# A sketched-attention and tanh-MLP kernel: loads of the last two batches held to half the bytes under way, and a new order on every engine

## The chip, the cores and the metric

The kernel runs on one core of a Trainium2 chip. The metric is the time of one execution on the device, in microseconds (us). Engines are named as the profile names them: PE is the matrix engine (PEld its weight loads), DVE the vector engine, ACT the scalar engine, POOL the GpSimd engine, SP the engine that asks for most transfers; DMA moves data between device memory and the on-chip memory, and PSUM is the memory of eight banks that matmuls write to.

## The reference

Two stages, cut to what matters. Shapes: q, k and v are 4 batches x 4 heads x 1088 positions x 32; the MLP takes 4352 tokens of 128 numbers through 2048 and back.

```python
def phi(x):                                    # S1, S2: 8 x 32
    a = einsum('rd,bhsd->bhsr', S1, x)
    b = einsum('rd,bhsd->bhsr', S2, x)
    return einsum('bhsi,bhsj->bhsij', a, b).reshape(..., 64)

q_p, k_p = phi(q), phi(k)
kv  = einsum('bhsf,bhsd->bhfd', k_p, v)
num = einsum('bhsf,bhfd->bhsd', q_p, kv)
den = einsum('bhsf,bhf->bhs', q_p, sum(k_p, axis=2))[..., None] + 1e-6
x   = (num / den).transpose(0, 2, 1, 3).reshape(4352, 128)
h   = x @ w_in                                 # 128 -> 2048
out = (h - tanh(h)) @ w_out                    # 2048 -> 128
```

## The kernel before

**Work.** A batch goes through these steps. Its k is transposed on DVE (`kT`), projected on PE by both sketches (L524), transposed back on DVE (`kab`, L534), and multiplied out to 64 features on POOL (`wk`, L567); PE forms a Gram matrix and a fold from it (L546, L556), by which the denominator comes out of the query projection, and then the sums over v (L593, or L652 for batches 2 and 3 in one). q is transposed (`qT`, L678), projected (L698), brought back (`qf`, L705) and turned into scaled features by DVE and POOL (`dt`, `den`, `rec`, `an`, `qp`, L711 to L734) and transposed again (`qpT`, L739). The numerators (L754) are matmuls of those with the sums; ACT copies the result as bf16 to `xT` (L771), which holds tokens along its columns.

The MLP takes tokens in twelve groups: 128, 128, 256, seven of 512, 128 and 128. For each 128 of the 2048 hidden units and a group of 512, one matmul of 512 columns writes h to one of the PSUM banks 4 to 6 (0 to 2 as well for the last groups) (L962), ACT makes tanh(-h) of it in bf16 (L968), and a second matmul adds its product with `w_out` to the output's bank 7 (L990). The linear part h @ w_out is not taken through the hidden units: `w_in @ w_out` is formed once (L933), split in two bf16 halves `whi` and `wlo`, and two matmuls (L1013) add x times them to the same bank. DVE moves a finished group's bank to `osb` (L1027), and SP stores it (L1034). Batch 0's first 256 tokens have a shorter way of their own (L782 to L874) so that the MLP can start early; matmuls on zeros (L1110), called fillers below, stand among these steps.

**Order.** The kernel records every step as an `Op` with its engine, its readers and writers, and from these finds the waits. The order on each engine is not worked out at build time: it is the table `ORDER`, a list of the numbers of the ops for each engine, and a negative number in PE's list stands for that many fillers (of 512 columns below -1000, else of 256). Each engine goes through its list in order and stops at an op whose input is not there, so everything that is listed behind it waits too. SP's list holds loads and stores alike.

**Loads.** `load` (L407) adds a rule of its own to each load by SP: going back over the loads that were recorded before it, it adds up bytes until its own and theirs exceed `AHEAD`, 1.9 MB, and makes the load wait for the landing of the one at which that happens. So at most about 1.9 MB is asked for and not landed. A due time goes with each load: below 20000 for batches 0 and 1 and the weights, 20000 to 40020 for k, v and q of batches 2 and 3. One k or q of a batch is 544 KB; v comes in four parts, three of 144 KB and one of 112 KB. k, q and v of batch 2 use the buffers of batch 0, those of batch 3 the buffers of batch 1.

Of the kernel before, what the change touches and what calls it, by code (L numbers as in the profile page):

```python
# [21 lines left out]
AHEAD = 1900000  # L22

ORDER = {
    "tensor": (
# [16 lines left out]
    ),  # L42
    "scalar": (
# [8 lines left out]
    ),  # L52
    "vector": (
# [5 lines left out]
    ),  # L59
    "gpsimd": (  # L60
        3, 20, 21, 4, 9, 22, 7, 8, 10, 75, 84, 82, 60, 59, 61, 62, 135, 133, 147, 148, 146, 283, 285, 305, 308, 306,
        309, 304, 307, 440, 442, 576, 578,
    ),
    "sync": (
# [4 lines left out]
    ),  # L69
}  # L70

# [256 lines left out]
def bass_polysketch_attn__then__act_tanh_shrink_kernel(nc, q, k, v, S1, S2, moe_w_in, moe_w_out, out):  # L328
# [78 lines left out]
    def load(eng, key, sem, due, fn, nbytes, also=False, rate=300, name="load"):  # L407

        o = P.op(eng, nbytes / rate, fn, w=() if also else key if isinstance(key, list) else [key], sem=sem, due=due,
                 name=name)  # L410
        if also:
            P.also(o, key)
        if eng == "sync":
            ahead, i = nbytes, len(flow)
            while i and ahead <= AHEAD:
                i -= 1
                ahead += flow[i][1]
            if ahead > AHEAD:
                landed[0] |= {flow[i][0]}
            o.deps |= landed[0]  # L420
            flow.append((o, nbytes))

    def load_s():
        for i, src in enumerate((S2, S1)):
            load("scalar", ("s_raw",), "s", 0, lambda e, i=i, src=src: e.dma_start(
                out=s_raw[8 * i:8 * i + 8, :, :], in_=src[:, None, :].to_broadcast([R, H, D])), 4096, True, name="load s")

    def load_k(b, due):
        cuts = ((0, 512), (512, S)) if b == 0 else ((0, S),)
        for x, (lo, hi) in enumerate(cuts):  # L430
            load("sync", [("kraw", b % 2, y) for y in ((x,) if b == 0 else (0, 1))], f"k{b}{x}", due, lambda e, lo=lo, hi=hi: e.dma_start(
                out=kraw[b % 2][:, lo:hi], in_=k[b].rearrange("h (j c) d -> (h j) (c d)", j=32)[:, lo:hi]),
                512 * (hi - lo), rate=400, name=f"load k{b}")

    def load_v(b, due):
        src = v[b].rearrange("h (j c) d -> j h c d", j=32)
        for x, c in enumerate((0, 2, 1, 3)):
            n = NT if c < 3 else 7
            load("scalar" if b == 0 and x % 2 else "sync", ("vx", b % 2), f"v{b}{c}", due + x, lambda e, c=c, n=n: e.dma_start(
                out=vx[b % 2][32 * c:32 * c + 32, :, 0:n, :].rearrange("j h t d -> j h (t d)"),  # L440
                in_=src[:, :, OFF[c]:OFF[c] + n, :].rearrange("j h t d -> j h (t d)")),
                128 * 128 * n, True, 226, name=f"load v{b}")
# [696 lines left out]
```

## Time and profile before

| | us |
|---|---|
| median of three runs | 106.21 |
| lowest and highest | 105.36 and 106.97 |
| the profiled execution, its own time | 105.88 |
| its span, from first to last instruction | 103.9 |
| PE busy in it | 94.4 |
| ACT busy in it | 81.5 |

The profile is of one execution. Line numbers (L962) are those of the kernel before. A row of the timeline gives the start, the length, the engine, the line, the operation with what it writes and reads, how many follow each other, and in brackets how long the engine sat idle ahead and what ended that. "issue" there means that the engine waited for nothing that the profile shows. PE's busy time counts matmuls whose ends are modelled and overlap, so a busy PE is not one at its fastest. In the list of transfers q1 is SP's queue and the kind "instruction" is the engines' own code being brought in.

### The profile page before, as it was taken

To read this page: it belongs to the slowest core of one execution; us is meant where nothing else is said; L and a number is where in the kernel's file an instruction comes from. 1 tells how busy PE (TensorE), PEld (TensorE's weight loads), DVE (VectorE), ACT (ScalarE), POOL (GpSimd) and SP (SyncE) were. 2 spreads that over 40 slices of the span, in tenths; PEclk is the share of its full clock that TensorE was granted. 3 is DMA by queue.
4 is the path that set the end of the run, shared out by engine and by line. 5 is a ranking of instruction groups with operands and counts; after the bars stand their busy time and mean duration, and the time that the engine had idled before them with its cause. 6 is when DMAs were issued, how large, how long until landed. Compare 5 with 4: busy or idle time off the path is not lost.

```text
span 103.9 us, 3200 instructions
## 1 busy us (share of the span) xinstructions
PE 94.4 (91%) x1353; PEld 51.9 (50%) x1364; DVE 56.4 (54%) x108; ACT 81.5 (78%) x173; POOL 32.9 (32%) x37
## 2 busy tenths in 40 slices
PE   5989998959689999999999999999999999999980
PEld 1336767737376444444845444344444323454770
DVE  3389879999595988069995307875320020020210
ACT  0528929725857979799689799999799999999960
POOL 5309042799300399995650000091000000000000
PEclk9999999999999999999999999999999999999999
DMA  2999999799962710033000420041005106014053
GB/s 46 318 246 397 396 347 248 246 239 271 284 203 65 193 23 0 6 51 50 6 0 3 73 32 0 14 66 27 0 6 81 20 9 92 0 21 69 14 84 68
DMA packets 22493, 11.21 MB, mean 108 GB/s; under 512 B 17872, under 2 KB 20304, under 8 KB 22480
## 3 DMA queue, kind: packets, MB, share of 16 engines
q1 hardware_dynamic: 21968, 10.69, 40.7%
q10 hardware_dynamic: 512, 0.34, 1.2%
q8 instruction: 10, 0.16, 0.7%
q14 instruction: 3, 0.02, 0.1%
HBM read 8.79 MB, written 2.23 MB: 106 GB/s over the span
## 4 chain that ended last, share of the span: by engine, by line
PE 50%; ACT 28%; DVE 6%; DMA 6%; SPq 3%; issue 3%; DVEq 0%
ACT tt L968 27%; PE ps L962 15%; PE ps L990 14%; DMA w_in_f<-in_moe_w_in_dram 6%; PE ps L754 6%; PE ps L698 3%; PE ps L1013 2%; PE ps L652 2%; PE ps L997 2%; DVE qpT L739 1%; SPq L452 1%; DVE kT L576 1%; PE ps L593 1%; PE ps L524 1%; PE ps L868 1%
## 5 line engine op out<-in xcount | busy, mean ns | idle before, releaser
L968 ACT ACTIVATE tt<-ps 128x512 bf16<-128x512 f32 x136 | 69.0, 685 | 6.8 <-PE ps L962 4.1
L962 PE MATMUL ps<-xT,w_in 128*128 128x512 bf16 (+2 forms) x184 | 42.1, 317 | 1.2 <-issue 0.7
L990 PE MATMUL ps<-tt,w_out 128*128 128x512 bf16 (+2 forms) x158 | 40.1, 336 | 1.8 <-issue 1.7
L962 PEld LDWEIGHTS ps<-xT,w_in 128*128 128x128 bf16 x192 | 18.0, 114 | 17.8 <-ACT tt L968 9.8
L990 PEld LDWEIGHTS ps<-tt,w_out 128*128 128x128 bf16 x160 | 14.2, 98 | 14.1 <-ACT tt L968 2.7
L1027 DVE STREAM_TRANSPOSE osb<-ps 128x512 f32<-128x512 f32 (+2 forms) x10 | 6.1, 605 | 26.3 <-PE ps L990 26.3
L734 POOL TENSOR_TENSOR qp<-an,qf 128x768 f32<-128x768 f32 (+1 forms) x8 | 11.7, 1458 | 25.3 <-DVE an L725 25.0
L567 POOL TENSOR_TENSOR wk<-kab 128x768 f32<-128x768 f32 x10 | 15.1, 1514 | 4.8 <-DVE kab L534 3.9
L739 DVE STREAM_TRANSPOSE qpT<-qp 128x768 f32<-128x768 f32 (+1 forms) x12 | 10.5, 903 | 0.8 <-POOL qp L734 0.8
L705 DVE STREAM_TRANSPOSE qf<-ps 128x1152 f32<-128x1152 f32 (+1 forms) x4 | 5.3, 1316 | 6.0 <-PE ps L698 6.0
L771 ACT CAST xT<-ps 128x272 bf16<-128x272 f32 (+2 forms) x12 | 4.0, 372 | 3.6 <-PE ps L754 3.4
L754 PE MATMUL ps<-qpT,ndw 32*32 32x272 f32 (+3 forms) x256 | 6.0, 385 | 0.3 <-ACT sw L583 0.3
L678 DVE STREAM_TRANSPOSE qT<-qraw 128x1088 f32<-128x1088 f32 (+2 forms) x5 | 5.3, 1062 | 0.5 <-DMA qraw<-in_q_dram 0.5
L1110 PE MATMUL ps<-wz 128*128 128x256 bf16 (+1 forms) x23 | 5.5, 373 | 0.0
L754 PEld LDWEIGHTS ps<-qpT,ndw 32*32 32x32 f32 x256 | 3.2, 103 | 2.5 <-DVE ndw L671 0.4
L1013 PE MATMUL ps<-xT,wlo 128*128 128x512 bf16 (+2 forms) x10 | 3.4, 338 | 1.1 <-DVE wlo L938 0.9
L898 POOL CAST w_out<-w_out_f 128x512 bf16<-128x512 f32 x4 | 2.4, 612 | 5.9 <-DMA w_out_f<-in_moe_w_out_dram 5.8
L771 DVE CAST xT<-ps 128x272 bf16<-128x272 f32 (+1 forms) x4 | 1.8, 511 | 4.5 <-ACT xT L771 2.3
L698 PE MATMUL ps<-qT,sw 32*32 32x288 f32 (+1 forms) x128 | 3.7, 399 | 0.1
L534 DVE STREAM_TRANSPOSE kab<-ps 128x288 f32<-128x288 f32 (+2 forms) x10 | 3.4, 391 | 0.6 <-PE ps L524 0.5
L1110 PEld LDWEIGHTS ps<-wz 128*128 128x128 bf16 x23 | 2.4, 114 | 2.4 <-issue 2.1
L734 DVE TENSOR_TENSOR qp<-ps,qf 128x768 f32<-128x768 f32 (+1 forms) x4 | 3.5, 881 | 0.0
(104 smaller groups left out, 79.0 us busy)
## 6 DMA issues: line engine op xcount, KB each, us to landing
kraw<-in_k_dram SPq DMA_DIRECT2D x3, 544.0 KB, 5.8
qraw<-in_q_dram SPq DMA_DIRECT2D x3, 544.0 KB, 5.4
vx<-in_v_dram SPq DMA_DIRECT2D x11, 144.0 KB, 5.3
out_dram<-osb SPq DMA_DIRECT2D x17, 64.0 KB, 2.0
w_in_f<-in_moe_w_in_dram SPq DMA_DIRECT2D x4, 256.0 KB, 5.8
w_out_f<-in_moe_w_out_dram SPq DMA_DIRECT2D x4, 256.0 KB, 5.7
qraw<-in_q_dram SPq DMA_DIRECT2D x1, 416.0 KB, 5.3
vx<-in_v_dram SPq DMA_DIRECT2D x3, 112.0 KB, 4.4
```

What stands on the lines that cost most here:

```text
L567: P.op(eng, dve(64 * n) if eng == "vector" else pool(64 * n), lambda e: e.tensor_tensor(out=wk[i][:, t0:t1, :, :, :].rearrange("p t h i j ...
L698: ins = e.matmul(ps[32 * c:32 * c + 32, h, 0:N], sw[32 * h:32 * h + 32, b, :], qT[i][32 * h:32 * h + 32, o:o + N], start=True, stop=True, ...
L734: e.tensor_tensor(out=qp[u][:, 4 * lo:4 * hi, :, :], in0=(pa if head else an[u][:, 4 * lo:4 * hi, :])[:, :, :, None].to_broadcast([128, m, ...
L739: P.op("vector", dve(64 * m), lambda e, lo=lo, hi=hi: e.transpose(out=qpT[u][:, :, 32 * lo:32 * hi].rearrange("p x (n j) -> p x n j", j=32 ...
L754: ins = e.matmul(ps[32 * h:32 * h + 32, c, 0:n], ndw[i][32 * c:32 * c + 32, y, 32 * h:32 * h + 32], qpT[u][32 * c:32 * c + 32, 2 * h + y, ...
L771: e.tensor_copy(dst, src) if on == "vector" else e.copy(dst, src), r=[bank[c]],
L962: ins = e.matmul(bk[:, n * y:n * y + n], w_tile(jb), xT[:, t0:t0 + n], start=True, stop=True)
L968: P.op("scalar", act(512), lambda e, ts=ts, bk=bk: e.activation(out=tt[:, ts, :], in_=bk, func=AF.Tanh, scale=-1.0), r=[kb], w=[("t", ts)] ...
L990: ins = e.matmul(acc[:, 0:n], w_out[:, jb, :], tt[:, ts, n * y:n * y + n], start=o.start and y == 0, stop=o.stop and y == per - 1)
L1013: P.op("tensor", 3 + n / 2.4, lambda e, o, x=x: e.matmul(acc[:, 0:n], x[:, :], xT[:, t0:t0 + n], start=o.start, stop=o.stop), r=[(nm,)] + ...
L1027: P.op("vector", dve(n), lambda e: e.transpose(out=osb[u][:, 0:n], in_=acc[:, 0:n]), r=[ka], w=[("osb", u, 0), ("osb", u, 1)], due=when(t0 ...
L1110: P.emit(lambda e, n: e.matmul(ps[:, 6, 0:n], wz[:, 0:128], wz[:, 0:n], start=True, stop=True))
```

## The change

Two things are changed. In `load`, the limit on the bytes under way is `AHEAD` for loads with a due time below 20000, as before, and half of it, 0.95 MB, for the others. And the table `ORDER` is a different one on every engine; 11 more fillers of 256 columns stand in PE's list. The steps themselves, their sizes and their engines are the same. The lines of the changed kernel stand one further down from L413 on.

```diff
         if eng == "sync":
             ahead, i = nbytes, len(flow)
-            while i and ahead <= AHEAD:
+            most = AHEAD if due < 20000 else AHEAD // 2
+            while i and ahead <= most:
                 i -= 1
                 ahead += flow[i][1]
-            if ahead > AHEAD:
+            if ahead > most:
                 landed[0] |= {flow[i][0]}
             o.deps |= landed[0]
             flow.append((o, nbytes))
```

Two lines of the table, PE's first:

```diff
-        2, -1005, -3, 47, -3, 65, 50, 80, -1, 68, -1, 69, -5, 94, 73, 93, 86, 103, 105, 96, 95, -5, 99, 124, 101, 110,
+        2, -1005, -3, 47, -3, 50, 65, 80, -3, 68, -1, 69, -4, 94, 73, -1, 103, 86, -1, 105, 95, 96, 93, -3, 124, 99,
```

What that makes of the order is shown at three places. The first is PE's list ahead of the first tanh: the last transposes of w_in (L920 before, L921 after), key sums of batch 0 (`wk,vx`), fillers (`wz`), query projection (`qT,sw`), the first numerators (`qpdT,kvd`), the turn of the sums (`ident,kvz`) and the first layer (`xT,w_in`). Before:

```order
L829 MATMUL ps<-qT,sw 32x256 x4
L920 MATMUL ps<-identb,w_in 128x128 x16
L811 MATMUL ps<-wk,vx 32x64 x16
L1110 MATMUL ps<-wz 128x256 x5
L868 MATMUL ps<-qpdT,kvd 32x128 x8
L698 MATMUL ps<-qT,sw 32x224 x16
L868 MATMUL ps<-qpdT,kvd 32x128 x8
L962 MATMUL ps<-xT,w_in 128x128 x12
L882 MATMUL ps<-ident,kvz 128x128 x2
```

After:

```order
L921 MATMUL ps<-identb,w_in 128x128 x8
L830 MATMUL ps<-qT,sw 32x256 x4
L1111 MATMUL ps<-wz 128x256
L921 MATMUL ps<-identb,w_in 128x128 x8
L812 MATMUL ps<-wk,vx 32x64 x28
L1111 MATMUL ps<-wz 128x256 x3
L699 MATMUL ps<-qT,sw 32x224 x16
L869 MATMUL ps<-qpdT,kvd 32x128 x16
L1111 MATMUL ps<-wz 128x256 x10
L883 MATMUL ps<-ident,kvz 128x128 x2
L963 MATMUL ps<-xT,w_in 128x128 x16
```

Half of the w_in transposes moved ahead, the query projection moved ahead of both numerators, and ten fillers and the turn now stand between the numerators and the first layer.

The second place is PE around the numerators of batch 0's other tokens (`qpT,ndw`): the Gram matrix (`kab`), the weight product (`w_out,w_inT`), the linear terms (`whi`, `wlo`), the fold (`zs,s2blk`), first layer (`xT,w_in`) and second layer (`tt,w_out`). Before:

```order
L933 MATMUL ps<-w_out,w_inT 128x128 x16
L546 MATMUL ps<-kab 32x32 x9
L1013 MATMUL ps<-xT,whi 128x128
L1013 MATMUL ps<-xT,wlo 128x128
L556 MATMUL ps<-zs,s2blk 32x8 x4
L754 MATMUL ps<-qpT,ndw 32x208 x32
L1013 MATMUL ps<-xT,wlo 128x128
L990 MATMUL ps<-tt,w_out 128x128 x16
L1013 MATMUL ps<-xT,whi 128x128
L962 MATMUL ps<-xT,w_in 128x256 x6
L698 MATMUL ps<-qT,sw 32x288 x16
```

After:

```order
L547 MATMUL ps<-kab 32x32 x9
L557 MATMUL ps<-zs,s2blk 32x8 x4
L934 MATMUL ps<-w_out,w_inT 128x128 x16
L755 MATMUL ps<-qpT,ndw 32x208 x32
L1014 MATMUL ps<-xT,wlo 128x128
L1014 MATMUL ps<-xT,whi 128x128
L963 MATMUL ps<-xT,w_in 128x256 x4
L991 MATMUL ps<-tt,w_out 128x128 x4
L1014 MATMUL ps<-xT,whi 128x128
L1014 MATMUL ps<-xT,wlo 128x128
L991 MATMUL ps<-tt,w_out 128x128 x8
L963 MATMUL ps<-xT,w_in 128x256 x2
```

The weight product moved behind the fold, directly ahead of the numerators; group 0's linear terms moved behind them; and first-layer matmuls of group 2 moved ahead of group 1's second layer, of which four more and then the query projection of batch 1 (32x288) follow.

The third is SP's list from the load of batch 1's q on, with what each waits for (`d_` the landing of the load of that name: `d_q1None` is all of q of batch 1, `d_v22` the second part asked for of v of batch 2, `d_k20` k of batch 2; `s_` an engine). Buffers ending in 0 take batch 2, those ending in 1 batch 3. Before:

```order
L447 DMA qraw1<-in_q_dram 128x1088 [waits d_k10]
L431 DMA kraw0<-in_k_dram 128x1088 [waits s_vector,d_wo3]
L439 DMA vx0<-in_v_dram 32x4x288 [waits s_tensor]
L439 DMA vx0<-in_v_dram 32x4x288 [waits d_v10]
L439 DMA vx0<-in_v_dram 32x4x288 [waits d_v12]
L439 DMA vx0<-in_v_dram 32x4x224 [waits d_v11]
L447 DMA qraw0<-in_q_dram 128x1088 [waits d_q1None,s_vector]
L1034 DMA out_0_dram<-osb0 32x4x32 [waits s_vector]
L431 DMA kraw1<-in_k_dram 128x1088 [waits d_k20]
L1034 DMA out_0_dram<-osb0 32x4x32 x3
L447 DMA qraw1<-in_q_dram 128x1088 [waits d_v21,s_vector]
```

After:

```order
L448 DMA qraw1<-in_q_dram 128x1088 [waits d_k10]
L432 DMA kraw0<-in_k_dram 128x1088 [waits d_q1None,s_vector]
L440 DMA vx0<-in_v_dram 32x4x288 [waits s_tensor]
L440 DMA vx0<-in_v_dram 32x4x288
L440 DMA vx0<-in_v_dram 32x4x288 [waits d_k20]
L440 DMA vx0<-in_v_dram 32x4x224
L448 DMA qraw0<-in_q_dram 128x1088 [waits d_v22,s_vector]
L1035 DMA out_0_dram<-osb0 32x4x32 [waits s_vector]
L1035 DMA out_0_dram<-osb0 32x4x32 x3
L1035 DMA out_0_dram<-osb1 32x4x32 [waits s_vector]
L1035 DMA out_0_dram<-osb1 32x4x32 x2
L432 DMA kraw1<-in_k_dram 128x1088 [waits d_q2None]
```

Each load of batches 2 and 3 now waits for a landing closer ahead of it: k of batch 2 for q of batch 1, q of batch 2 for a part of v of batch 2, k of batch 3 for q of batch 2; and seven stores stand between the last two.

More of the change, by code (lines that the diff above doesn't have):

```diff
@@ L60 @@
     "gpsimd": (
-        3, 20, 21, 4, 9, 22, 7, 8, 10, 75, 84, 82, 60, 59, 61, 62, 135, 133, 147, 148, 146, 283, 285, 305, 308, 306,
-        309, 304, 307, 440, 442, 576, 578,
+        3, 21, 20, 9, 4, 7, 10, 8, 22, 84, 75, 82, 59, 60, 61, 62, 135, 133, 147, 146, 148, 283, 285, 308, 305, 306,
+        309, 307, 304, 440, 442, 578, 576,
     ),
```

60 rows, old and new, of the table ORDER are left out of this document.

## The prediction

> **What bounds the kernel now.** I read the page first, then the 5 us windows, then the chain of waits where the windows show the matrix engine (PE) short of work, then the transfers there. Of the page:
>
> ```profile
> span 103.9 us, 3200 instructions
> PE 94.4 (91%) x1353; PEld 51.9 (50%) x1364; DVE 56.4 (54%) x108; ACT 81.5 (78%) x173; POOL 32.9 (32%) x37
> PE 50%; ACT 28%; DVE 6%; DMA 6%; SPq 3%; issue 3%; DVEq 0%
> q8 instruction: 10, 0.16, 0.7%
> L968 ACT ACTIVATE tt<-ps 128x512 bf16<-128x512 f32 x136 | 69.0, 685 | 6.8 <-PE ps L962 4.1
> ```
>
> Two engines share the bound: PE first, the 136 tanh of ACT at the end. "issue", waiting for nothing that the profile shows, has 3% of the chain, and q8 carries instructions: ten packets, 0.16 MB. The windows say where each engine has room:
>
> ```profile
> 20.00:25.00 5.00, 3.71 (x120) 2.72 (x118) 5.00 (x9) 1.50 (x6) 4.70 (x4) 1.00 0.91 252
> 25.00:30.00 5.00, 3.86 (x65) 2.92 (x63) 3.78 (x6) 3.41 (x9) 1.81 (x2) 1.00 0.94 305
> 30.00:35.00 5.00, 4.82 (x97) 3.22 (x96) 3.86 (x7) 4.26 (x9) 0.00 (x0) 1.00 0.36 98
> 75.00:80.00 5.00, 5.00 (x25) 2.42 (x24) 0.72 (x1) 5.00 (x12) 0.00 (x0) 1.00 0.24 35
> ```
>
> (PE, its weight loads, DVE, ACT, POOL, clock, DMA share, GB/s.) The clock is granted in full. PE is short of 1.29 and 1.14 us between 20 and 30 us, where DMA is over nine tenths busy, and of 0.18 just after. From 75 us ACT is full. What PE gains before 35 us moves everything behind it forward, as long as PE and ACT keep their pace. The chain, and the idle times of PE's weight loads and of ACT:
>
> ```profile
> 22.35 0.23 PE ps L1013
> 23.05 1.32 PE ps L754 x60
> 27.62 0.11 PE ps L990
> 27.73 1.14 issue
> 28.87 0.42 PEld L990 LDWEIGHTS ps<-tt,w_out 128*128 128x128 bf16 x4 [1.32 <-issue]
> 29.83 1.57 ACT L968 ACTIVATE tt<-ps 128x512 bf16<-128x512 f32 x3 [1.53 <-PE ps L962]
> ```
>
> For 1.3 us PE issues nothing, and ACT loses 1.5 us behind it. Cut at this gap, at the earlier one that ends at 14.57 us, and where about 256 instructions (matmuls plus weight loads) lie between cuts, the same view gives:
>
> ```profile
> 9.60:14.57 4.97, 4.71 (x144) 3.11 (x135) 4.20 (x13) 3.89 (x7) 2.16 (x4) 1.00 1.03 391
> 14.57:23.04 8.47, 6.84 (x127) 5.20 (x127) 7.99 (x17) 5.02 (x12) 4.66 (x5) 1.00 0.91 254
> 23.04:27.46 4.42, 4.41 (x127) 3.24 (x128) 3.20 (x5) 2.95 (x8) 3.69 (x3) 1.00 0.92 265
> 27.46:28.87 1.41, 0.27 (x4) 0.09 (x1) 1.41 (x2) 0.84 (x2) 0.00 (x0) 1.00 1.00 310
> 36.70:42.10 5.40, 5.05 (x136) 2.60 (x129) 3.91 (x7) 4.39 (x11) 4.96 (x5) 1.00 0.05 9
> ```
>
> 127 and 128 between 23.04 and the gap: PE has eaten a block of some 256 and waits for the next. Each stretch holds one q8 packet. In the stretches 26.4 to 26.5 and, in a quiet time, 37.3 to 37.4 the transfers are:
>
> ```profile
> q1 hardware_dynamic: 20, 0.02, 64.0%
> q8 instruction: 1, 0.02, 58.7%
> ...
> q8 instruction: 1, 0.02, 60.2%
> ```
>
> So I read: when a block is begun, the next one is asked for; its packet starts 0.6 us later when DMA is quiet (36.7 to 37.3), but 3.4 us later with q1 full (23.04 to 26.4), and is of use at 28.87, 5.8 us after the asking; the earlier one took 14.57 - 9.60 = 5.0 us.
>
> [...]
>
> **The change, part by part.**
>
> *Front, to the first tanh.* Before:
>
> ```profile
> 12.55 0.72 PE L1110 MATMUL ps<-wz 128*128 128x256 bf16 x5
> 14.58 0.80 PE L868 MATMUL ps<-qpdT,kvd 32*32 32x128 f32 x16
> 15.32 0.86 PE L962 MATMUL ps<-xT,w_in 128*128 128x128 bf16 x12
> ```
>
> After, the first weight transpose stands before the last key sums, so the block boundary of 9.6 us is crossed some 0.45 us later; plus 5.0 that is 15.05, in the middle of the first numerators. I take 0.65 for the rest of them (0.80 for half), 1.2 for ten filler matmuls (0.72 for five, whose tails overlap), 0.3 for the turn that now stands ahead: first layer at 17.2 instead of 15.32. This 1.9 us is covered, up to what follows: batch 1's numerators (L754, 23.05) waited for DVE's transposes and ACT's sketch copy. After: 17.2 + 0.45 to the first tanh + 8 tanh at 0.51 (69.0/136) + copies and fold 0.4 = 22.25, then the weight product 0.95: 23.2. On DVE's side the query projection now precedes both numerators, which brings the transposes some 0.4 forward: 22.65 at best. I take +0.15, from -0.4 to +0.6.
>
> *The two linear terms of group 0* stood before L754, one hiding in a wait (22.35 row), and now stand behind it: +0.15.
>
> *First layer before group 1's second layer.* Behind L754 PE did 16 small second-layer matmuls while ACT copied x; now four first-layer matmuls stand first and wait for the second copy:
>
> ```profile
> 24.41 1.29 ACT L771 CAST xT<-ps 128x208 bf16<-128x208 f32 x4 [1.43 <-PE ps L754]
> ```
>
> Half of 1.29 is 0.65 behind L754's end, of which the linear terms fill 0.15: +0.5.
>
> *The fetch.* By count, the boundary that was crossed at 23.04 now lies in the weight product, before L754's wait, near 22.4. The next lies near the end of batch 1's query projection, which PE reaches at 23.2 + 4.4 (the row's 4.42, since both hold a block) = 27.6, plus about 0.2 as the mix of matmuls differs: 27.8. So 5.4 us lie between, where there were 4.4. With 5.0 or less no wait is left; with 5.8 as now, 0.4. At that time the throttle leaves 0.85 MB under way or less (k and half of v of batch 2). I take no wait: -1.3, from -0.9.
>
> Sum: 0.15 + 0.15 + 0.5 - 1.3 = -0.5.
>
> *The throttle itself.* Rows of SP's queue and of the landings:
>
> ```profile
> 18.35 0.35 SPq L431 DMA_DIRECT2D kraw<-in_k_dram  x1
> 23.95 0.35 SPq L431 DMA_DIRECT2D kraw<-in_k_dram  x1
> kraw<-in_k_dram SPq DMA_DIRECT2D x3, 544.0 KB, 5.8
> qraw<-in_q_dram SPq DMA_DIRECT2D x1, 544.0 KB, 5.6
> kraw<-in_k_dram SPq DMA_DIRECT2D x1, 256.0 KB, 2.8
> ```
>
> (The 5.6 is q of batch 1, asked for at 15.84.) k of batch 2 now waits for that landing, 21.4 instead of 18.35; q of batch 2 waits for half of v, k of batch 3 for q. The loads stand one behind another, with less ahead of each. A load of 544 KB alone I estimate at 2.8 + 288 KB at the 391 GB/s of the 9.60 row = 3.5 us. Then k2 lands at 24.9, v at 25.9, q2 at 29.6, k3, asked at 29.8 behind the stores, at 33.3. DVE's place for k3's transpose comes behind these:
>
> ```profile
> 33.05 0.45 DVE L1027 STREAM_TRANSPOSE osb<-ps 128x256 f32<-128x256 f32 x1 [1.11 <-PE ps L990]
> 33.43 0.38 DVE L610 COPY ndw<-ps 128x256 f32<-128x256 f32 x1
> 35.09 0.34 DVE L725 TENSOR_TENSOR an<-qf,rec 128x192 f32<-128x192 f32 x1
> ```
>
> near 33.9, as PE, 0.3 to 0.5 ahead, still feeds them. So it costs nothing with 0.6 us to spare; bounds: nothing, and what landings of 5.6 would cost (below). Queued behind that wait on DVE is the factor product of batch 1 (L725, 35.09 now, near 35.3 then), which POOL waits for; k3's late sibling v3 and q3 are read after 39 us.
>
> Behind 35 us the matrix engine's kinds of work stand with about the same count of first-layer tiles per unit of work, and the tanh are the same 136: I take 0, give or take 0.6.
>
> The profiled execution took 105.88 us (103.9 and 2.0 around it); the median of three is 106.21, all four average 106.1. 106.1 - 0.5 = **105.6**.
>
> **Rivals.**
>
> *The chain of loads becomes the bound (slower).* Each us that a landing is longer counts three times (k2, q2, k3), less the 0.6. At 3.7 us per landing it is even; at 4.5, midway to 5.6 and 0.9 to 1.0 more than 3.5, k3 comes 3.0 later, 2.4 of it felt: 108.0; at 4.6 it is over 2% slower, at 5.6 6.3 - 0.6 = 5.7: 111.3. For it: 5.6 and 5.8 are all that loads of this size show. Against: these had three to four others ahead of them, and 144 KB of v landed in 2.8 with little ahead:
>
> ```profile
> vx<-in_v_dram SPq DMA_DIRECT2D x3, 144.0 KB, 2.8
> ```
>
> *The fetch stays as late as now* (any full ring holds it up, half as many bytes help nothing): 5.8 us, 0.4 left, 106.1 - 0.1 = 106.0. [...]
>
> *The stall is no fetch*, so it stays: without the -1.3, 106.9. The counts and packets speak against it.
>
> *More gain*: L754 at 22.65, and nothing of the 0.5 felt: -0.4 - 1.3 = -1.7, so 104.4; and the later order takes from ACT's waits, of which this is the longest, up to 1.2 more: 103.2.
>
> ```profile
> 52.37 5.25 ACT L968 ACTIVATE tt<-ps 128x512 bf16<-128x512 f32 x10 [1.37 <-PE ps L652]
> ```
>
> Against: the key sums (L652) stand as they did, only two first-layer tiles sooner.
>
> **How the numbers follow.** Forecast 0.48 (105.0 to 106.3: the spread of its terms, most of which offset each other); fetch as late 0.14; no fetch 0.06; chain of loads 0.16, of it 0.09 over 2%; more gain 0.16, of it 0.12 over 2%. The range leaves out most of the more gain and the worse half of the load chain: 104.1 to 107.7. 2%, about what a measurement tells from no change, is 104.1 and 108.3: faster 0.12, same 0.79, slower 0.09.
>
> **What would show it.** Right: no "issue" gap of 1 us on PE near 28 us, L754 near 23.2, the first tanh near 17.6, landings of k and q near 3.5 us, kT of batch 3 on DVE near 34 us. Wrong: a wait of DVE for k or q between 25 and 36 us, a gap of PE at another 256th instruction, or L754 past 23.8.

## The result and the profile after

The changed kernel took **109.38 us** (median of six, 108.50 to 109.46) against 106.14 for before on the same chip: ratio 1.034, 95% interval 1.027 to 1.040, slower. The forecast was 105.6, with a range to 107.7. Times below are medians in us, and "before" beside them is the kernel before on the same chip. Ratios, and the median spans in the part on the experiments, leave disturbed executions out, so that a ratio can differ from the quotient of the medians.

The page of the changed kernel (an execution of 108.50 us; here and below, code behind L413 has numbers one higher than in the kernel before, so L755 is the L754 of the prediction):

```profile
span 106.3 us, 3233 instructions
PE 98.3 (93%) x1375; PEld 53.6 (50%) x1375; DVE 56.5 (53%) x108; ACT 81.7 (77%) x173; POOL 33.1 (31%) x37
PE 58%; ACT 20%; DMA 9%; SPq 5%; DVE 2%; issue 2%; DVEq 0%
q8 instruction: 11, 0.18, 0.7%
kraw<-in_k_dram SPq DMA_DIRECT2D x3, 544.0 KB, 4.5
qraw<-in_q_dram SPq DMA_DIRECT2D x3, 544.0 KB, 3.8
```

DMA has risen from 6 to 9% of the chain and SP's queue from 3 to 5, there are eleven packets of code instead of ten, and a landing of k takes 4.5 us instead of 5.8 (medians of three). Rows of PE's timeline (start, length, engine, line, operation, in brackets the idle time ahead and its end):

```profile
15.20 0.84 PE L869 MATMUL ps<-qpdT,kvd 32*32 32x128 f32 x19 [0.60 <-issue]
15.97 1.27 PE L1111 MATMUL ps<-wz 128*128 128x256 bf16 x10
17.30 0.83 PE L963 MATMUL ps<-xT,w_in 128*128 128x128 bf16 x12
23.46 1.33 PE L755 MATMUL ps<-qpT,ndw 32*32 32x208 f32 x64
25.59 0.63 PE L963 MATMUL ps<-xT,w_in 128*128 128x256 bf16 x4 [0.57 <-ACT xT L772]
27.36 1.55 PE L699 MATMUL ps<-qT,sw 32*32 32x288 f32 x32
36.78 1.21 PE L525 MATMUL ps<-kT,sbd 64*32 64x288 f32 x32 [0.33 <-DVE kT L618]
45.82 0.77 PE L699 MATMUL ps<-qT,sw 32*32 32x288 f32 x32
```

The wait for code in the front, the ten fillers, the first layer, the numerators and the copy's wait stand nearly where the prediction put them. Not as forecast: the query projection of batch 1 lasts 1.55 us, twice the 0.77 of its sister at 45.82 (the wait for code is still there, inside it; the run e8 below shows it as idle time), and the key projection of batches 2 and 3 at 36.78 waits for DVE. SP's asking, DVE's wait, and the last store, which before was issued in 0.65 us at 100.99:

```profile
21.19 0.35 SPq L432 DMA_DIRECT2D kraw<-in_k_dram  x1
27.16 0.38 SPq L448 DMA_DIRECT2D qraw<-in_q_dram  x1
30.91 0.43 SPq L432 DMA_DIRECT2D kraw<-in_k_dram  x1
102.30 1.89 SPq L1024 DMA_DIRECT2D out_dram<-osb  x1
35.41 1.31 DVE L618 STREAM_TRANSPOSE kT<-kraw 128x1088 f32<-128x1088 f32 x1 [0.61 <-DMA kraw<-in_k_dram]
```

The comparison that turned out to matter is the first and last row of tanh on ACT. Before:

```profile
15.77 2.06 ACT L968 ACTIVATE tt<-ps 128x512 bf16<-128x512 f32 x4 [2.21 <-PE ps L962]
74.47 26.10 ACT L968 ACTIVATE tt<-ps 128x512 bf16<-128x512 f32 x53
```

and after:

```profile
17.77 2.56 ACT L969 ACTIVATE tt<-ps 128x512 bf16<-128x512 f32 x5
74.93 27.08 ACT L969 ACTIVATE tt<-ps 128x512 bf16<-128x512 f32 x55
```

So a span has three parts: the start of the first tanh, the stretch to the end of the last, and the rest. Before: 15.77 + 84.80 + 3.4; after: 17.77 + 84.24 + 4.25. The first tanh is 2.0 later and the rest 0.9 longer; only 0.6 of it comes back in the stretch, although the 1.3 us gap of before stood in that stretch. The stretch holds 136 tanh (69 us), ACT's copies (5) and its idle time (10).

### The profile page after: what moved, and what is told of

It is laid out like the page before. It is cut to its first block, busy times and chain, and to the rows that moved or that the text cites. A ratio compares the mean times of both kernels' runs of the same rounds, so it can differ in the third digit from the quotient of the medians.

```text
span 106.3 us, 3233 instructions
## 1 busy us (share of the span) xinstructions
PE 98.3 (93%) x1375; PEld 53.6 (50%) x1375; DVE 56.5 (53%) x108; ACT 81.7 (77%) x173; POOL 33.1 (31%) x37
## 4 chain that ended last, share of the span: by engine, by line
PE 58%; ACT 20%; DMA 9%; SPq 5%; DVE 2%; issue 2%; DVEq 0%
PE ps L963 19%; PE ps L991 17%; ACT tt L969 17%; DMA w_in_f<-in_moe_w_in_dram 5%; DMA kraw<-in_k_dram 4%; PE ps L755 4%; SPq L1035 3%; PE ps L1014 2%; PE ps L653 2%; PE ps L699 2%; PE ps L998 2%; PE ps L525 2%; PE ps L1111 2%; PE ps L869 1%; ACT xT L772 1%
## 5 line engine op out<-in xcount | busy, mean ns | idle before, releaser
L963 PE MATMUL ps<-xT,w_in 128*128 128x512 bf16 (+2 forms) x192 | 44.9, 320 | 1.0 <-ACT xT L772 0.6
L991 PE MATMUL ps<-tt,w_out 128*128 128x512 bf16 (+2 forms) x160 | 41.6, 337 | 0.0
L1111 PE MATMUL ps<-wz 128*128 128x256 bf16 (+1 forms) x34 | 7.5, 353 | 0.0
L755 PE MATMUL ps<-qpT,ndw 32*32 32x272 f32 (+3 forms) x256 | 6.0, 385 | 0.0
L1111 PEld LDWEIGHTS ps<-wz 128*128 128x128 bf16 x34 | 3.4, 111 | 3.2 <-issue 2.7
L755 PEld LDWEIGHTS ps<-qpT,ndw 32*32 32x32 f32 x256 | 3.2, 103 | 1.8 <-issue 0.9
```

Source lines behind the costliest of these rows:

```text
L755: ins = e.matmul(ps[32 * h:32 * h + 32, c, 0:n], ndw[i][32 * c:32 * c + 32, y, 32 * h:32 * h + 32], qpT[u][32 * c:32 * c + 32, 2 * h + y, ...
L963: ins = e.matmul(bk[:, n * y:n * y + n], w_tile(jb), xT[:, t0:t0 + n], start=True, stop=True)
L991: ins = e.matmul(acc[:, 0:n], w_out[:, jb, :], tt[:, ts, n * y:n * y + n], start=o.start and y == 0, stop=o.stop and y == per - 1)
L1111: P.emit(lambda e, n: e.matmul(ps[:, 6, 0:n], wz[:, 0:128], wz[:, 0:n], start=True, stop=True))
```

## The experiments

The same sum for every profile, worked out from such pairs of rows (one execution each). With it stand the start of the numerators (L754 or L755 near 23 us, those of batch 0's other tokens, which the prediction calls batch 1's), the landing of batch 3's k (k3; k2 and q2 are those of batch 2) and the length of the first key projection (the L524 or L525 row near 6 us), which the last part of this document needs:

| kernel | first tanh | numerators | stretch | rest | span | k3 landed | L524 row |
|---|---|---|---|---|---|---|---|
| before | 15.77 | 23.05 | 84.80 | 3.38 | 103.9 | 29.7 | 0.72 |
| changed | 17.77 | 23.46 | 84.24 | 4.25 | 106.3 | 35.4 | 0.72 |
| changed, again (e8) | 17.37 | 23.07 | 85.54 | 4.13 | 107.0 | 36.3 | 0.72 |
| old order, limit halved (e1) | 17.53 | 24.46 | 87.56 | 3.38 | 108.5 | 34.1 | 1.21 |
| new order, full limit (e2) | 19.10 | 24.79 | 83.19 | 4.23 | 106.5 | 35.0 | 1.21 |
| before, 20 more (e3) | 15.83 | 22.79 | 83.17 | 3.39 | 102.4 | 28.2 | 0.72 |
| changed, 160 more (e4) | 18.12 | 23.87 | 83.25 | 3.32 | 104.7 | 34.7 | 1.21 |
| changed, 4 fewer (e5) | 16.83 | 22.53 | 86.35 | 4.30 | 107.5 | 36.6 | 0.72 |
| changed, no ten fillers (e6) | 15.79 | 22.32 | 87.07 | 3.32 | 106.2 | 36.1 | 0.72 |
| before, ten fillers (e7) | 16.56 | 23.48 | 83.14 | 3.38 | 103.1 | 28.6 | 0.97 |
| new order, full limit, no ten (e9) | 17.25 | 23.00 | 83.25 | 3.32 | 103.8 | 32.9 | 0.72 |
| before, 30 more (e10) | 17.88 | 24.80 | 83.37 | 3.39 | 104.6 | 29.2 | 1.21 |
| changed, 12 fewer (e11) | 19.14 | 24.83 | 83.20 | 3.31 | 105.7 | 35.6 | 1.21 |
| 1.4 MB, no ten (e12) | 18.60 | 24.30 | 83.40 | 3.33 | 105.3 | 35.4 | 0.72 |
| before, finer fillers (e13) | 15.56 | 22.66 | 83.74 | 3.38 | 102.7 | 29.2 | 0.72 |
| as e9, finer fillers (e14) | 16.74 | 22.81 | 83.87 | 3.32 | 103.9 | 32.9 | 0.72 |

"More" and "fewer" are PE instructions. Single profiles vary (first tanh by over 1 us), so the argument goes by parts, and by medians over several executions.

**The limit alone (e1).** In the old order, `most = AHEAD if due < 20000 else AHEAD // 2` as in the change.

> The order of before with the halved limit. Theory A (the changed kernel's 3.2 us come from several small places, of which the limit owns only the late k of batch 3): the landings are those of the changed kernel (k2 near 25.3, k3 near 35.4), DVE waits 0.5 to 1.5 us for k3, the fetch gap at 28 us shrinks by up to 0.6 since less is under way: 106.3 to 107.3 us. Rival B (the chain of loads is nearly the whole loss): 108.5 to 109.5. Rival C (the limit costs nothing, all is in the order): 105.5 to 106.2.

Measured: 111.13, before 105.89, ratio 1.051 (1.039 to 1.063): more than any of the three had. Rows of DVE and PE:

```profile
34.15 1.31 DVE L618 STREAM_TRANSPOSE kT<-kraw 128x1088 f32<-128x1088 f32 x1 [2.48 <-DMA kraw<-in_k_dram]
36.60 0.88 PE L991 MATMUL ps<-tt,w_out 128*128 128x512 bf16 x2 [2.55 <-DVE osb L1028]
```

And a row of the windows (PE, its weight loads, DVE, ACT, POOL, clock, DMA share, GB/s):

```profile
36.80:40.21 3.41, 3.41 (x9) 1.22 (x8) 2.58 (x5) 1.22 (x3) 0.72 (x1) 0.50 0.89 218
```

DVE stands at k3's transpose for 2.5 us, and the move of a finished group out of bank 7, which is listed behind it, makes PE wait as long: the queue behind a waiting instruction. The chain of loads, a rival of the prediction, is real. Not all of the 5 us is that wait: behind it the clock was granted at 0.50 for 3.41 us, and the 512-column matmuls start every 0.43 instead of 0.22 us. Counted from the numerators, the 21st tanh is 3.2 us later than in e3 below, the 25th 4.4, and the last still 4.4. This profile also began with slow first matmuls (last section), which put its first tanh at 17.53. In the new order the group's move stands ahead of the transpose, and the limit costs less there (e9, e14).

**The new order alone (e2).**

```diff
-            most = AHEAD if due < 20000 else AHEAD // 2
+            most = AHEAD
```

> The new order with the full limit of 1.9 MB. Theory A: the wait for k3 is gone (0.5 to 1.0 us less), but the tail (last store issued for 1.9 us) stays, the copy bubble stays, and the fetch gap in the query projection near 27 us is as long or longer (0.8 to 1.4): 107.8 to 109.0 us. Rival B: 105.8 to 106.4. Rival C: 109.0 to 109.8.

Measured: 109.01, before 105.89, ratio 1.031 (1.022 to 1.040). In its profile neither the wait for k3 nor the gap in the query projection is left (stretch 83.19), but the first tanh is at 19.10, after slow first matmuls, and the rest is 4.23. So without its limit the change loses nearly as much, at another place, and part of that front may be chance. The time is at the upper edge of theory A, whose gap in the query projection did not come. SP asks for k3 no earlier than 31.11 here (28.77 in e9 below), behind the seven stores, where before asked at 23.95: the order of SP's list alone makes k3 land at 35.0, and DVE, which takes it up at 35.41, just has no use for it sooner.

**Where the boundaries lie (e3, e10, e13).** In before, PE instructions are added in the first fillers, so every block of code (254 instructions of PE from 14.57 to 23.04 us in before, 255 from there to 27.46) ends that much earlier in the work: 11 or 16 tiny matmuls (32 columns) for one filler of 512 columns, or the same columns cut finer. A filler is two instructions, a weight load and a matmul (34 of each at L1111 in the changed kernel), so that 11 for one make 20 more, not the 22 that the expectations say.

```diff
-        2, -1005, -3, 47, -3, 65, 50, 80, -1, 68, -1, 69, -5, 94, 73, 93, 86, 103, 105, 96, 95, -5, 99, 124, 101, 110,
+        2, -1004, -2011, -3, 47, -3, 65, 50, 80, -1, 68, -1, 69, -5, 94, 73, 93, 86, 103, 105, 96, 95, -5, 99, 124, 101, 110,
```

> Before with 22 more PE instructions at the start (11 tiny matmuls for one filler of 512 columns): every boundary of 256 comes 22 instructions earlier in the work, and the work itself is unchanged. Fetch theory: the 1.1 us gap at 27.73 moves into batch 1's query projection (near 26.4) and shrinks to 0.2 to 0.7 us, since the block holds 5.5 us instead of 4.8; and an eleventh q8 packet shows near 101 us, with the last store's issue stretched from 0.65 to 1.5 us or more. Sum -0.6 + 1.0: 106.2 to 107.2 us. No fetch theory: gap where it was, no eleventh packet, 106.1 us.

> Before with 30 more PE instructions at the start (16 tiny matmuls for one filler of 512 columns). Boundaries and front as with 22 more, but the last boundary lies 46 instructions before the end instead of 16 or 36. Tail theory (a boundary crossed early enough before the end brings an eleventh packet onto the last store): packet near 100 us, the last store's issue 1.7 to 1.9 us, PE's end to span end 3.8 instead of 2.9: 0.9 above the run with 22 more, 105.7 to 107.5 us. Rival (that packet belongs to something else in the new order): tail 2.9, 104.8 to 106.6 us.

> Before with the first fillers cut finer (512 columns to two of 256, 256 to two of 128): the same columns in the same place, 22 PE instructions more, no tiny matmuls. Fetch theory: the gap of 1.1 us at 27.7 is gone as in the run with 22 more, and PE is kept as busy as before at the start, so that fewer executions have the slow first matmuls: span 102.2 to 103.0 in most executions, 104.6 to 105.4 us. If the wide spread of the runs with 22 and 30 more (spans 102.2 to 105.9) belongs to the shifted boundaries and not to the tiny matmuls, the spread is here too: median 105.8 to 106.6.

Measured: 106.46 (before 105.89, ratio 0.996, 0.990 to 1.002), 106.56 (105.84, 1.000, 0.992 to 1.008) and 105.61 (106.24, 0.998, 0.994 to 1.003). In all three profiles the gap at 27.7 us is gone and the stretch is 83.2 to 83.7 instead of 84.8 (the last of them has a new gap of 0.6 at 21.4). In e3 the first gap now stands inside batch 0's query projection, its boundary 20 instructions earlier in the work:

```profile
14.42 0.41 PE L698 MATMUL ps<-qT,sw 32*32 32x224 f32 x6 [0.69 <-issue]
22.79 1.32 PE L754 MATMUL ps<-qpT,ndw 32*32 32x208 f32 x64 [0.29 <-ACT sw L583]
```

The gaps move with the count of instructions, so they are waits for code, as the prediction had them. The medians gain nothing measurable: executions spread from 104.6 to 108.2, and the two speeds of the first matmuls (last section) may be the reason, since e10's profile has the slow one and a span of 104.6, the two others the fast one and 102.4 and 102.7. That a PE kept busy at the start makes the slow one rarer, as e13's expectation has it, was my estimate and was not shown: e13's spans still reach from 102.7 to 105.4. The packet at the end, expected in e3 and e10, came in neither, so that e3's time lies in its range by luck; e13's lies between its two ranges.

**Boundaries in the changed kernel (e4).** 85 tiny matmuls for the five fillers of 512 columns.

> The changed kernel with 160 more PE instructions at the start (85 tiny matmuls for five fillers of 512 columns). By the trace of the changed kernel cut at the new places, the blocks before 32 us then last 6.1, 6.3 and 5.4 us instead of 4.8, 7.5 and 4.8, and no boundary falls into the last 8 us. Fetch theory: no gap at 15 us (0.6), none or 0.3 us left at 24 us for the 0.8 at 27, and the last store's issue is short again (-0.9): 106.8 to 107.8 us. No fetch theory: 109.0 to 109.8 us, gaps where they were.

Measured: 108.17, before 105.89, ratio 1.024 (1.015 to 1.032), just above the range expected. No wait for code over 0.2 us is left and the rest is 3.32, but the first key projection took 1.21 instead of 0.72 us and the first tanh came at 18.12.

**The changed kernel once more (e8).**

> The changed kernel as it is, once more: what differs between its executions. If the first fetch sets it, a profile of a 109.3 us execution shows the q8 packet of the front near 14 instead of 12.84 us, the first tanh 0.8 to 1.3 us later than 17.77, and the rest as it was. If it is spread over the run, the first tanh is within 0.3 us.

Measured: 109.18, before 105.41, ratio 1.038. The profiled execution took 109.49, and the first fetch is not its difference: the first tanh was even earlier, and the time was lost behind it. SP, DVE and PE:

```profile
28.11 0.35 SPq L448 DMA_DIRECT2D qraw<-in_q_dram  x1
32.28 0.68 SPq L432 DMA_DIRECT2D kraw<-in_k_dram  x1
31.78 1.31 DVE L679 STREAM_TRANSPOSE qT<-qraw 128x1088 f32<-128x1088 f32 x1 [0.51 <-DMA qraw<-in_q_dram]
36.30 1.31 DVE L618 STREAM_TRANSPOSE kT<-kraw 128x1088 f32<-128x1088 f32 x1 [0.99 <-DMA kraw<-in_k_dram]
28.15 0.67 PE L699 MATMUL ps<-qT,sw 32*32 32x288 f32 x4 [0.42 <-issue]
```

q2 was asked for at 28.11 (27.16 in the first profile), k3 at 32.28 behind seven stores, and DVE waits for both. The last row is the end of batch 1's query projection: it lasts from 26.97 to 28.82, 1.1 us longer than the 0.77 of its sister, with a wait for code inside.

**Without the ten fillers (e6), and with them in before (e7).**

```diff
-        101, -10, 137, 108, 110,
+        101, 137, 108, 110,
```

> The changed kernel without the ten fillers ahead of its first layer. Start theory (a later first tanh is paid in full, since tanh, copies and idle times behind it come to 83.2 us in every order without fetch gaps): first tanh 1.0 to 1.3 us earlier than with them at the same fetch, the same 83 to 84.3 us from the first to the last tanh, and the tail short (20 instructions less): 1.9 to 2.2 us less, 107.0 to 107.9 us. Rival of my prediction (a late start is covered, as the numerators at L755 wait for DVE and ACT anyway): the stretch from first to last tanh grows by the 1.2 us, only the tail is won: 108.1 to 108.8 us.

> Before with ten fillers of 256 columns put ahead of its first layer, which delays the first tanh by 1.1 to 1.3 us and shifts the later boundaries by 20 instructions, as in the run with 22 more. Start theory: first to last tanh 83.0 to 83.4 us as there, first tanh near 16.9 to 17.1 (at the same fetch): 105.9 to 107.3 us, 0.8 to 1.3 above the run with 22 more at the same first fetch. Rival (covered): the stretch shrinks to 82.0 to 82.4, 104.8 to 106.2 us.

Measured: e6 108.26, before 105.41, ratio 1.029 (1.022 to 1.036). The first tanh came 1.6 to 2.0 us earlier than in the two profiles of the changed kernel, and the last tanh ended at 102.86 as if nothing had been won (102.01 and 102.90 in those two). What holds it is in the chain of waits, cut to 15 to 39 us with some pieces left out:

```profile
15.47 5.63 DMA qraw<-in_q_dram
21.12 5.65 DMA kraw<-in_k_dram
26.78 0.31 SPq L440
27.67 4.81 DMA qraw<-in_q_dram
32.51 1.31 DVE qT L679
35.37 0.37 DVE osb L1028
37.69 1.13 PE ps L525 x32
```

The chain of loads from q of batch 1 on, and nothing of PE or ACT in 17 us of it. DVE is late with q2, and behind it with a group's move, for which PE stands idle 2.08 us from 33.71 on. My start theory failed here by its number, but not in kind: the earlier start is hidden by the loads, not by the numerators' wait that the prediction named. In before, where no load is late, e7 shows the start theory: 105.93, before 105.41, ratio 1.012 (1.001 to 1.022); against e3, the first tanh is 0.73 later (16.56 against 15.83), the numerators 0.69 (23.48 against 22.79), the stretch is the same 83.1 to 83.2 and the span 0.7 longer. The time lies in the ranges of both theories; the stretch decides between them.

**Both away (e9, e14), and half the limit's step (e12).** The new order with 1.9 MB and without the ten fillers; e14 has 8 PE instructions more; e12 has 1.4 MB.

> The new order with the full limit of 1.9 MB and without the ten fillers ahead of the first layer: beside the run without the fillers (108.26) only the limit differs. Load theory (q of batch 1, k2, q2, k3 one behind another hold the projection of batches 2 and 3 at 37.6 whatever the start): without the chain, k3 lands near 32, that projection starts near 33.8 (18.0 behind a first tanh near 15.8, as in the order alone), first to last tanh 83.2 to 84.0, tail short: 104.6 to 106.0 us. Rival (the chain is worth only the wait of 0.3 to 0.6 us that the first profile of the changed kernel showed): 107.3 to 108.0 us.

> The new order with the full limit, without the ten fillers ahead of the first layer, and with four of the 512-column fillers cut in two (8 PE instructions more than without, 2779 by my count, still without the packet at the end). With a first tanh at 15.8 (fetch wait 0.4 to 0.8 us in the front) the sum is 15.8 + 83.2 + 3.4 = 102.4 of span, 104.7 us; with the wait of 1.7 that the profile without the ten fillers and with 1.9 MB had, 103.8. If its executions spread over both, the new order as such costs nothing and what is left against before is the front's fetch: median 104.7 to 106.5 us. If the order as such costs 1 us or more: first to last tanh over 84 us, median above 106.8.

> The changed kernel without the ten fillers and with a limit of 1.4 MB for batches 2 and 3, between 0.95 and 1.9: k2 then waits for a part of v of batch 1 instead of its q, q2 for k2, and k3 for nothing that is late. Load theory: k3 lands at 32 to 33.5, the projection starts at 33.8 to 35.0: 104.8 to 106.6 us. Rival (half as many bytes or fewer under way is what counts, in proportion): halfway between the runs with 0.95 and 1.9 MB. Rival (the limit hardly matters): 107.3 to 108.3.

Measured: e9 107.83 (106.19 to 108.80; before 105.84, ratio 1.026, 1.015 to 1.037), a miss by 1.8 us; e14 106.46 (before 106.24, ratio 1.015, 1.007 to 1.022); e12 106.87 (before 105.84, 1.012, 1.002 to 1.022), 0.3 above its range. The chain is gone (k3 lands at 32.9 in e9 and e14, at 35.4 in e12, where DVE waits 0.39 us for it; stretch 83.3 to 83.9), and the rest is short. But the front was not as lucky as in e6. Rows of e9, then of e12, and the window behind the latter:

```profile
15.73 0.84 PE L869 MATMUL ps<-qpdT,kvd 32*32 32x128 f32 x19 [1.69 <-issue]
```

```profile
16.04 1.49 PE L869 MATMUL ps<-qpdT,kvd 32*32 32x128 f32 x19 [1.85 <-issue]
15.89:19.30 3.41, 3.27 (x34) 2.68 (x34) 2.52 (x7) 1.07 (x3) 1.23 (x2) 0.50 0.92 229
```

e9 waits 1.69 us for code there, where e6, with the same instructions on PE, waited 0.39. e12 waits 1.85 us, and then the clock is granted at 0.50 for 3.41 us: the same 19 matmuls take 1.49 instead of 0.84, and the first tanh comes at 18.60. The device time also held 3.6 and 3.7 us around the span in two of e9's four runs, where most others have 1.9 to 2.6; so spans are the better measure here. Median span: changed kernel 107.0 (10 runs), e11 105.7, e6 106.0, e2 106.5 (with the long end), e9 and e14 together 104.05 (8 runs), e12 104.3, before 103.25 (30 runs). **Taking away the limit alone or the fillers alone wins little (0.5 us at e2; nothing from e11 to e6); taking away both wins 1.65 us more than the short end alone (105.7 to 104.05).** They lie on two paths of about the same end, each hiding the other. That the loads hide the fillers is plain in the profiles: in the six with the new order and the halved limit, the last tanh ends at 101.4 to 103.2 us for a first tanh anywhere from 15.79 to 19.14. That the fillers hide the loads is less sure, as it rests on e2, whose profile has the slow first matmuls.

**The end (e5, e11).** Two of the first fillers fewer (e5), and six fewer (e11, whose edit this is).

```diff
-        2, -1005, -3, 47, -3, 50, 65, 80,
+        2, -1003, -1, 47, -1, 50, 65, 80,
```

> The changed kernel with two of its first three 256-column fillers left out, which leaves PE 4 instructions less (2788 by my count instead of 2792). Tail theory (past a length between 2789 and 2792 the last boundary asks for one block more, and that packet falls on the last store): no q8 packet past 100 us, the last store's issue near 0.65 us instead of 1.89, PE's end to the end of the span 2.9 us instead of 3.8: 0.9 us less than the changed kernel, 108.1 to 108.8 us. Rival (the long issue has another cause, such as the order of SP's list): packet and tail stay, 109.0 to 109.6 us.

> The changed kernel with six early fillers left out, which leaves PE 12 instructions less (2780 by my count, between the 2772 that showed no packet at the end and the 2788 that did). Tail theory: no q8 packet near 103, last store's issue 0.65 us; the front may start earlier, but the loads hold the projection of batches 2 and 3 at 37.0 to 38.0: 0.9 less than the changed kernel, 107.9 to 108.7 us. If packet and tail stay: 108.8 to 109.6.

Measured: e5 108.96 (before 105.41, ratio 1.038, 1.030 to 1.045), packet and long end still there; e11 107.99 (before 105.84, ratio 1.027, 1.016 to 1.038), both gone. The last store of e11:

```profile
102.62 0.64 SPq L1024 DMA_DIRECT2D out_dram<-osb  x1
```

In all 16 profiles, the four with a q8 packet at 102 to 104 us (changed, e2, e5, e8) issue the last store in 1.75 to 1.93 us and have a rest of 4.1 to 4.3; the twelve others take 0.64 or 0.65 and have 3.3 to 3.4. So this is 0.9 us, and it belongs to a packet of code that runs while the last store is asked for. When it comes is open. By my count of PE's instructions, the new order has it at 2788 and 2792; at 2772 (e6, e9, e12) the traces show a packet 1.0 to 1.7 us after the last instruction, where it costs nothing; at 2779 and 2780 (e14, e11) none at all. The old order has none at 2799 (e10), and one behind the end in e7.

## Why the prediction was wrong

- **Front to the first layer: right in time, wrong in price.** Forecast code at 15.05, first layer at 17.2, first tanh at 17.6, numerators at 23.2 (the terms given for them add up to 23.1); measured 15.20, 17.30, 17.77, 23.46 (14.81, 16.90, 17.37, 23.07 in e8). **The step that failed is "This 1.9 us is covered".** The numerators came near the forecast, but not because a delay is absorbed ahead of them. Within one order they move with the start. The rows of e10 (old order) and e11 (new order):

```profile
24.80 1.32 PE L754 MATMUL ps<-qpT,ndw 32*32 32x208 f32 x64 [0.29 <-ACT sw L583]
```

```profile
24.83 1.33 PE L755 MATMUL ps<-qpT,ndw 32*32 32x208 f32 x64
```

  e10's first tanh is 2.05 us later than e3's, and its numerators 2.01, with the same wait of 0.29 ahead of them. With the new order they follow the first tanh by 5.7 us in eight profiles; only the two earliest starts (e6, e14) leave PE a wait there, of 0.35 and 0.14 us. With the old order it is 6.9 to 7.3. So the new order gets there 1.2 us sooner after the first tanh, with the same eight tanh made by then, but with other work, such as group 0's linear terms, left for later. That comes back: from the numerators to the end of the last tanh it takes 77.5 to 77.8 us in the profiles of the new order whose loads are late by 0.4 us at most (e2, e4, e9, e11, e12, e14), and 76.2 to 76.6 in those of the old order without the gap at 27.7 (e3, e7, e10, e13). From first to last tanh these ten have the same 83.1 to 83.9 us, for first tanh from 15.56 to 19.14: a late start is paid in full, unless something later holds the end anyway.
- **Linear terms and the copy's wait: right in place (0.57 for the forecast 0.5), too small in price.** I had put 0.15 and 0.5 for what the new order does behind the numerators; the difference above is 1.3. Some 0.8 of it is there by the 13th tanh; where the rest arises was not traced.
- **The fetch: -1.3 forecast, less gained.** The boundary moved as counted, but the next block still came late: 0.8 us lost inside the query projection, 1.1 in e8. That was the rival with 0.4 left. Without the limit the same gap was not there in e2, whose front came later; the time of a packet varies from run to run (that of the front started at 11.82 us in e6 and at 13.27 in e9, with the same list on PE).
- **The throttle: 0 forecast, and its 0.6 us to spare was used up.** The rival "chain of loads" was at work, with 0.16. Forecast landings of 3.5 us, v 1.0 behind k2, k3 at 33.3; measured in e8 k2 3.9, the asking for q2 2.5 behind k2's landing (the part of v that it waits for took 5.5), q2 3.6, k3 asked 0.5 behind it, as SP was still busy with the seventh store, whose issue took 0.89 us beside a packet of code, and landed after 4.0, at 36.3. So 3.0 us later than forecast: 1.8 of it between the loads and 0.9 in the landings of k2 and k3. Behind the numerators it costs about 0.3 us in the first profile, 1.2 in e8 and 3.0 in e6, which starts earliest: a late start hides a part of it.
- **"Behind 35 us: 0"** held for the work, but not for the end: 0.9 us for the eleventh packet, which the prediction did not name. I had counted the boundaries in the front only. (DVE also waits for q of batch 3, 1.17 us at 42.55 in the first profile; it costs nothing, as from the 25th tanh on that profile keeps its distance to e9 within 0.1 us.)
- **What adds up.** In the prediction's terms, against the profile of before:

| term | forecast | changed (108.50) | again (e8) |
|---|---|---|---|
| numerators | +0.15 | +0.4 | 0.0 |
| the order behind them | +0.65 | +1.3 | +1.3 |
| gap of before, new wait for code | -1.3 | -1.3 + 0.75 | -1.3 + 1.1 |
| loads | 0 | +0.3 | +1.2 |
| end | 0 | +0.9 | +0.75 |
| sum | -0.5 | +2.3 | +3.1 |

By the medians of the span the change costs 3.75 us: 1.3 of it goes with twelve instructions fewer (107.0 to 105.7: the end, and in the profile of e11 the gap in the query projection too), 1.65 with the ten fillers and the limit, and 0.8 is left.

In ten of the profiles PE waits 0.3 to 1.85 us for code ahead of the first layer (0.60 in the changed kernel, 1.69 in e9, 1.85 in e12).

What stays open: the rule of the last packet, and 0.8 us of span between the new order without its three costs (104.05) and before (103.25). In e9 and e14 the first tanh came 1.0 to 1.5 us later than in before. The packet of code that PE waits for there started at 13.27 and 12.83 us, against 12.20 in before, but at 11.82 in e6, which has e9's list on PE; so chance has a part in it, and that this is all of it was not shown. The new lists of DVE, ACT and POOL were never run without that of PE. No kernel tried is measurably faster than before: e13 comes closest, at 0.998 (0.994 to 1.003).

## What to carry to other kernels

When one engine has a fixed sum of work, price a change in its start by that engine's whole stretch (first to last tanh here), not by whether the next shared wait still comes at the same time: a new order may get there sooner because it leaves work for later. Two late paths that meet hide each other: undoing one shows little, so undo both before acquitting either. With fewer bytes under way most landings here were shorter (k 4.5 instead of 5.8 us, q 3.8 instead of 5.4, the larger parts of v 4.4 instead of 5.3; medians), but parallel loads became a chain, whose hops on the asking queue (stores and other loads listed between) add to the transfers: 2.5 and 0.5 us in e8.

## What was not expected of the hardware

**The first matmuls run at two speeds, and the windows of the profile show the same clock for both.** The first key projection of the changed kernel, and of e2, which has the same instructions up to there:

```profile
6.22 0.72 PE L525 MATMUL ps<-kT,sbd 64*32 64x288 f32 x16
```

```profile
6.57 1.21 PE L525 MATMUL ps<-kT,sbd 64*32 64x288 f32 x16
9.93 1.25 PE L1111 MATMUL ps<-wz 128*128 128x256 bf16 x5
```

(The last row is of e1.) 0.72 or 1.21 us for the same work, and the windows print a granted clock of 1.00 for both; in e1 a filler still takes 0.25 us at 10 us, where it takes 0.15 in the changed kernel at 8.5 (0.61 for four). The trace's own record of the clock does tell them apart: in these profiles it begins with full speed (at 5.9 us in the changed kernel), and the windows print 1.00 where it has nothing (from 0 to 5 us there). It begins at 4.3 to 5.9 us in ten profiles, all with 0.72, and at 9.9 to 13.5 in the five with 1.21 (e7, with 0.97, has no record). The first tanh of those five lies at 17.5 to 19.1, that of the ten at 15.6 to 17.8, but for e12 with its 18.60, where the clock fell back to 0.50 for 3.41 us. This may be much of the spread of before itself (104.6 to 107.9), of which one execution was profiled. In e1, still slow at 10 us, PE's first matmul was at 1.26; what sets the moment of full speed was not tested.

**The clock was halved beside some waits of PE, and not beside others as long.** It was granted at 0.50 for 3.41 us behind a wait of 2.55 us (e1) and from the end of one of 1.85 us on (e12), and stayed at 1.00 beside waits of 1.69 us (e9) and 2.08 us (e6). What decides it was not tested.

**Where SP took over 0.9 us to ask for a transfer, a packet of code was on its way.** SP's issue of the last store took 1.89 instead of 0.65 us while a packet ran (102.35 to 103.73 us, in the changed kernel), and that of a part of v 1.41 us (at 25.66 there, beside the packet of 25.42 to 26.69) instead of 0.4 elsewhere. In the 16 profiles SP issues 72 transfers behind 11 us that take over 0.9 us, of 1137, and every one of them overlaps a packet of code.
